# Top-k attention followed by a low-rank mixer: the division by the row sums made on transposed values, with the inverse sums passed through DRAM

## The chip, the cores and the metric

The kernel runs on one core of a Trainium2 chip. A core has five engines, each with its own in-order queue: TensorE (PE, matmuls and transposes; PEld is its weight load), VectorE (DVE), ScalarE (ACT), GpSimd (POOL) and SyncE (SP, which here only issues DMAs). They meet through semaphores. Data lies in SBUF (128 partitions), matmul results in PSUM, inputs and outputs in DRAM. The metric is the device time of one execution in microseconds (us); lower is better.

## The reference

Batch 8, 8 heads, 576 positions, head size 64, everything fp32. Attention keeps the 32 largest scores of each row; its output, with the heads side by side, goes through a mixer over positions (rank 32 between U and V) and a two-layer MLP.

```
scores = scale * np.matmul(q, k.transpose(0, 1, 3, 2))
kth = np.partition(scores, -top_k, axis=-1)[..., -top_k:-top_k + 1]
scores = np.where(scores >= kth, scores, -1000000000.0)
scores = scores - np.max(scores, axis=-1, keepdims=True)
attn = np.exp(scores)
attn = attn / (np.sum(attn, axis=-1, keepdims=True) + 1e-09)
o = np.matmul(attn, v)

x = o.transpose(0, 2, 1, 3).reshape(B, S, H * D)
h = x.transpose(0, 2, 1) @ U @ V
u = x + h.transpose(0, 2, 1)
out = u + np.maximum(u @ w_ch1, 0.0) @ w_ch2
```

w_ch1 is 512 x 2048 and w_ch2 is 2048 x 512.

## The kernel before

Two heads make a pair `g`: 4 pairs per batch, 32 in all. The 576 rows of a pair are five row tiles: t = 0 to 3 of 128 rows (`MAIN` = 512) and a tail, t = 4 (`NT`), of 64 rows, in which both heads share one tile (head 0 in partitions 0 to 63, head 1 in 64 to 127). The first four pairs (g < `NPAIR`) take five steps, one per tile; from pair 4 on a pair takes four steps, and the last of them holds t = 3 and the tail.

Each tile passes through these stages, spread over four successive steps:

- `scores` (TensorE, L332 and for the tail L364; ScalarE copies into `Ssb` at L377 to L400), `fold` and `split`, which make from each row two shorter ones (`pair`: GpSimd sum at L428, VectorE maximum at L430, GpSimd difference at L431).
- `front`: VectorE finds the 32nd largest value by MAX8 and MATCH_REPLACE8 (L481 to L516). Then ScalarE and GpSimd (L542 to L546) push all smaller scores far down, and ScalarE takes the exponential and, with it, the row sums (`weigh`, L435). The row sums of a pair are the columns of `den`: rows are partitions, and the nine columns are 4 tiles x 2 heads and the tail. 1e-9 is added at L556.
- The probabilities are turned. From pair 6 on (`shared`) the main tiles go through `blocks`: VectorE transposes 32x32 blocks into `y` (L572), SyncE writes `y` to DRAM (`away`, L578), and `back` reads it as `PT` on ScalarE's queue (L587). Tails are turned by TensorE (`turns`, L608 and L613).
- `values`: TensorE multiplies by v. For t < 4 the result has features in partitions and rows in columns (`O`, L646 and L649; ScalarE copies it into `XT` at L658). For the tail the rows stay in partitions (L633), and ScalarE scales both halves by the inverse row sum on the way into `x` (L641).
- `mixed`, once per pair: TensorE turns `XT` back to rows (L672), ScalarE copies to `x` (L676), GpSimd multiplies by the inverse row sums (L677, `den4`), TensorE multiplies by U into `pT` (L688), ScalarE copies it (`Tb`, L696), then for two parts of the columns TensorE multiplies by V (L700) and adds `x` by turning it onto the same PSUM tile (L702). ScalarE copies the sum into `uT` (L710), which has features in partitions. `inverse` (L621) makes the reciprocal on VectorE.

When the fourth pair of a batch is mixed, `mlp(b)` is put on the list of fillers: first layer L742, with the ReLU copy `hT` at L755, second layer L760, `uT` added on GpSimd at L772, and the result turned back (L784) and written out (L790). The last batch goes through `closing`, a second way to make the same products with fewer matmuls (L829 to L1041), which runs after all attention work.

The order on every engine is written out by hand: the loop at the end of the kernel goes through the steps and calls parts of `front` (a generator), `scores`, `values` and so on. `fill()` stands between them some seven times a step; each call moves `mixed` by one `yield` and then issues MLP matmuls until a fixed share of work (`share`, in units of matmul columns) is paid out. `mixed(g, None, 1)` waits one `fill`, does the first part, and goes on in the next step.

PSUM tiles come from three pools of two buffers: `ps_s` (scores), `ps_m` (MLP) and `ps_t` (`O`, `tp`, `pT`, `up`). A DMA's completion is counted on one of eight semaphores, and the build makes a DMA wait until the earlier DMA on its semaphore has landed, whichever queue issued that.

Of the kernel before, what the change touches and what calls it, by code (L numbers as in the profile page):

```python
# [8 lines left out]
F32 = mybir.dt.float32  # L9
# [3 lines left out]
ALU = mybir.AluOpType  # L13
# [13 lines left out]
def kernel(  # L27
# [28 lines left out]
    nc = tc.nc  # L56
    B, H, S, D = q.shape
    P = 128
# [4 lines left out]
    NT, TAIL = 4, 64  # L63
    MAIN = NT * P
    HALF = S // 2
    assert S == MAIN + TAIL and D == 64 and H % 2 == 0 and C == 512 and TOPK % 8 == 0
    NPAIR = H // 2
    NP = B * NPAIR

    CH = NT + 1  # L70
    ALONE = NPAIR * CH
# [4 lines left out]
    BLK = 32  # L76
# [4 lines left out]
    const = ctx.enter_context(tc.tile_pool(name="const", bufs=1))  # L81
# [22 lines left out]
    vds = [const.tile([P, P], F32, name=f"vd{i}") for i in range(NV)]  # L104
    vts = [const.tile([P, 2, D], F32, name=f"vt{i}") for i in range(NV)]

    xs = [const.tile([P, NT + 1, P], F32, name=f"x{i}") for i in range(2)]
    for i in range(NV):
        nc.gpsimd.memset(vds[i], 0.0)
        nc.gpsimd.memset(vts[i], 0.0)  # L110
    for x in xs:
        nc.gpsimd.memset(x[:, NT, :], 0.0)
    W1Q = F // NT
    w1s = [const.tile([P, NC, W1Q], F32, name=f"w1{i}") for i in range(NT)]
    w2 = const.tile([P, NF, C], F32, name="w2")
    U = const.tile([P, NT + 1, R], F32, name="U")

    V = const.tile([NT * R, S], F32, name="V")
    four = const.tile([P, 1], F32, name="four")
    nc.vector.memset(four, -4.0)  # L120

# [8 lines left out]
    def cols(t):  # L130
        return slice(t * P, t * P + rows(t))

    def at(t):
        return slice(OFF[t], OFF[t] + rows(t))

    def half(h):
        return slice(h * D, (h + 1) * D)
# [96 lines left out]

    raw, qkTs, S2s, uTs, XTs, dens = {}, {}, {}, {}, {}, {}
    probs, PTs, folds, fronts_of = {}, {}, {}, {}
    inverted, aways = set(), {}

    def load(g):

# [376 lines left out]
    def inverse(g, lo, hi):  # L617
        den = dens[g][:, lo:hi]
        if g == NPAIR - 1:
            nc.vector.tensor_scalar_add(den, den, 1e-9)  # L620
        nc.vector.reciprocal(den, den)  # L621

    def values(g, t):

        PT = PTs.pop((g, t))
        va, vd, vt = (a[g % NV] for a in (vas, vds, vts))
        O = ps_t.tile([P, P], F32, tag="tp", name="O")
        if t == NT:
            den, x = dens[g], xs[g % 2]
            if g not in inverted:  # L630
                inverse(g, 2 * NT if g == NPAIR - 1 else 0, 2 * NT + 1)
            for j in range(NT + 1):
                nc.tensor.matmul(  # L633
                    O,
                    lhsT=PT[:, j],
                    rhs=va[:, :, j, :] if j < NT else vt,
                    start=(j == 0),
                    stop=(j == NT),
                )
            for h in range(2):  # L640
                nc.scalar.mul(x[half(h), NT, half(h)], O[half(h), half(h)], den[half(h), 2 * NT :])  # L641
            return
        if shared(g, t):
            PT = PT.rearrange("p c n -> p (c n)")
            PT = PT.rearrange("p (a c j) -> p c a j", a=4, j=BLK)
        nc.tensor.matmul(O, lhsT=vd, rhs=PT[:, 2 * NT], start=True, stop=False)  # L646
        for j in range(NT):
            for h in range(2):
                nc.tensor.matmul(  # L649
                    O[half(h)],  # L650
                    lhsT=va[:, h, j, :],
                    rhs=PT[:, NT * h + j],
                    start=False,
                    stop=(j == NT - 1),
                )
        if t == 0:
            XTs[g] = attn.tile([P, MAIN], F32, tag="XT", name="XT", bufs=1)
        nc.scalar.copy(XTs[g][:, cols(t)], O)  # L658


    def mixed(g, wait, lag=0):

        for _ in range(lag):
            yield
        b, gi = divmod(g, NPAIR)
        if gi == 0:
            uTs[b] = mlpp.tile([P, NC, S], F32, tag="uT", name="uT")
        XT, den = XTs.pop(g), dens[g]
        X = xs[g % 2]
        tp = ps_t.tile([P, NT, P], F32, tag="tp", name="tp")  # L670
        for t in range(NT):
            nc.tensor.transpose(tp[:, t, :], XT[:, cols(t)], ident)  # L672
        X4 = X[:, 0:NT, :].rearrange("p t (h d) -> p t h d", h=2)
        tp4 = tp.rearrange("p t (h d) -> p t h d", h=2)
        den4 = den[:, 0 : 2 * NT].rearrange("p (t h) -> p t h ()", h=2).to_broadcast([P, NT, 2, D])
        nc.scalar.copy(X4, tp4)  # L676
        nc.gpsimd.tensor_tensor(X4, X4, den4, ALU.mult)  # L677
        if wait is None:
            waiting.append(g)
            while g in waiting:  # L680
                yield
        else:
            for _ in range(wait):
                yield
        pT = ps_t.tile([P, P], F32, tag="tp", name="pT")
        for t in range(NT + 1):
            i = t % NT * R
            nc.tensor.matmul(  # L688
                pT[i : i + R, :],
                lhsT=U[:, t, :],  # L690
                rhs=X[:, t, :],
                start=(t < NT),
                stop=(0 < t),
            )
        Tb = mlpp.tile([P, P], F32, tag="Tb", name="Tb")
        nc.scalar.copy(Tb, pT)  # L696
        yield
        for chunks, (lo, hi) in zip(PARTS, SPAN):
            up = ps_t.tile([P, WIDE], F32, tag="tp", name="up")
            nc.tensor.matmul(up[:, 0 : hi - lo], lhsT=Tb, rhs=V[:, lo:hi], start=True, stop=False)  # L700
            for t in chunks:
                nc.tensor.matmul(  # L702
                    up[:, OFF[t] - lo : OFF[t] - lo + rows(t)],
                    lhsT=X[:, t, :],
                    rhs=ident if t < NT else ident2,
                    is_transpose=True if t < NT else None,
                    start=False,
                    stop=(t == chunks[-1]),
                )
            nc.scalar.copy(uTs[b][:, gi, lo:hi], up[:, 0 : hi - lo])  # L710
            yield
        if gi == NPAIR - 1:
            fillers.append(closing(b) if b == B - 1 else mlp(b))
# [343 lines left out]
    STEPS = len(steps)  # L1057
# [27 lines left out]
    def tiles(n):  # L1085

        return steps[n] if 0 <= n < STEPS else []

    def weighted(m):

        for g, t in reversed(tiles(m)):
            values(g, t)
        if tiles(m)[-1][1] == NT:
            mixing.append(mixed(g, None, 1) if m < STEPS - 1 else mixed(g, 5, 0))
# [6 lines left out]
    def turned(n):  # L1101

        for g, t in tiles(n):
            yield from turns(g, t)
# [9 lines left out]
    for n in range(STEPS + 2):  # L1114
# [99 lines left out]
        turn()  # L1214
        fill()
        next(last, None)
        next(here, None)
        next_params(1)
        fill()
        if n >= STEPS:  # L1220
            weighted(n - 2)
        elif n - 2 >= ALONE and len(tiles(n - 2)) > 1:
            g2 = steps[n - 2][0][0]
            inverted.add(g2)
            inverse(g2, 0, 2 * NT + 1)
        next(here, None)
        bound = tiles(n + 1)[:1] == [(NPAIR + 1, 0)]
        if not bound:
# [7 lines left out]
        for tile_ in tiles(n - 1):  # L1236
            if shared(*tile_):
                blocks(*tile_)
        turning = turned(n - 1)
        if n < STEPS and t < 2 and g + 1 < NP:  # L1240
            if t == 0:
                coming = loading(g + 1)
            next(coming)
# [41 lines left out]
```

## Time and profile before

| | us |
|---|---|
| three runs | 1685.37, 1685.62, 1686.76 |
| median | 1685.62 |
| the profiled execution | 1686.28 |
| its span (first to last instruction) | 1684.5 |
| TensorE busy | 1586.0 (94%) |
| VectorE busy | 1543.7 (92%) |
| ScalarE busy | 1000.1 (59%) |
| GpSimd busy | 939.0 (56%) |
| mean of the 16 DMA engines, over the span | 107 GB/s |

The profile was taken from one execution. Its page gives busy time by engine, the span in 40 slices with the granted TensorE clock, and the chain of waits followed back from the last instruction; the trace behind it can be asked for any stretch, for one engine's timeline, or for the instructions of one line. A row of a timeline is: start, length, engine, line, operation, output <- inputs, number of merged instructions, and in brackets the idle time before with what ended it. "PEq", "SPq", "ACTq" are the engines' queues issuing a DMA or waiting. In the profile one fp32 matmul shows as two MATMUL records, and a transpose as one.

The span falls into four parts: up to about 280 us the first batch, with the weights being unpacked; from there to about 1540 us the pairs 4 to 31, four steps each; then the rest of the MLP before; and from 1570 us `closing`.

### The profile page before, as it was taken

The page shows a single profiled execution, that of the slowest core. Times are in us where ns is not written, and L with a number is a line of the kernel's source. Part 1 is how long each engine was busy: PE and PEld are TensorE (multiplying, and loading weights), DVE is VectorE, ACT ScalarE, POOL GpSimd, SP SyncE. Part 2 cuts the span into 40 slices and gives each one's busy share as a digit, 9 for nine tenths or more (in the row PEclk, how much of TensorE's full clock was granted, in tenths as well). Part 3 has the DMA queues.
Part 4 walks back from the last instruction along what each step waited for, and adds up shares of the span by engine and source line. Part 5 has one row for each costly group of instructions (what it writes and reads, how often), then busy time and mean ns, then how long its engine had stood idle before and what let it go on. Part 6 is the DMA issues. An engine that isn't in the chain of part 4 may idle for free.

```text
span 1684.5 us, 29512 instructions
## 1 busy us (share of the span) xinstructions
PE 1586.0 (94%) x9498; PEld 1213.4 (72%) x9498; DVE 1543.7 (92%) x4364; ACT 1000.1 (59%) x2475; POOL 939.0 (56%) x741
## 2 busy tenths in 40 slices
PE   4666799999899999999999999999999999999999
PEld 2444466788677887788777887778777887778876
DVE  7999998999999999999999999999999999994452
ACT  4888778665665656565665656565665656554320
POOL 4778668655555555555555555555555455552620
PEclk7788799999999999999999999999999999999999
DMA  3323232254545555554545555554545455533001
GB/s 87 96 75 96 58 91 73 55 133 123 131 110 136 125 131 128 131 129 120 128 117 130 125 130 125 132 125 125 128 115 131 122 134 124 131 105 102 10 1 29
DMA packets 273898, 180.97 MB, mean 107 GB/s; under 512 B 171376, under 2 KB 258256, under 8 KB 273744
## 3 DMA queue, kind: packets, MB, share of 16 engines
q1 hardware_dynamic: 257712, 117.49, 30.2%
q10 hardware_dynamic: 16032, 61.61, 11.7%
q8 instruction: 75, 1.23, 0.3%
q14 instruction: 79, 0.65, 0.1%
HBM read 108.23 MB, written 70.78 MB: 106 GB/s over the span
## 4 chain that ended last, share of the span: by engine, by line
PE 54%; DVE 32%; SPq 4%; DMA 4%; issue 2%; POOL 2%; ACT 1%; DVEq 0%; ACTq 0%; POOLq 0%
PE mm L760 16%; PE mm L742 16%; DVE m L516 10%; DVE upper L511 9%; PE sc L332 4%; PE O L649 4%; DVE first L498 3%; PE mm L836 3%; DVE y L572 3%; DVE upper L483 2%; PE sc L836 2%; PE tp L836 2%; DVE place L511 2%; DMA ld<-in_k_dram 2%; SPq L255 2%
## 5 line engine op out<-in xcount | busy, mean ns | idle before, releaser
L742 PE MATMUL mm<-uT,w 128*128 128x320 f32 (+1 forms) x1792 | 461.1, 410 | 1.9 <-ACT hT L755 1.9
L760 PE MATMUL mm<-hT,w 128*128 128x320 f32 (+1 forms) x1792 | 461.5, 408 | 0.0
L546 POOL TENSOR_TENSOR Ssb<-Ssb,E 128x576 f32<-128x576 f32 x243 | 339.4, 1416 | 210.7 <-ACT E L545 210.4
L742 PEld LDWEIGHTS mm<-uT,w 128*128 128x128 f32 x1792 | 333.7, 191 | 97.5 <-issue 12.0
L760 PEld LDWEIGHTS mm<-hT,w 128*128 128x128 f32 x1792 | 330.5, 190 | 90.3 <-issue 10.2
L516 DVE MAX8 m<-upper 128x8 f32<-128x304 f32 (+1 forms) x780 | 367.4, 512 | 0.7
L511 DVE MATCH_REPLACE8 upper<-m,upper 128x304 f32<-128x304 f32 (+1 forms) x520 | 259.9, 507 | 0.0
L431 POOL TENSOR_TENSOR lower<-lower,upper 128x576 uint32<-128x576 uint32 x108 | 152.3, 1410 | 157.5 <-DVE upper L430 152.6
L428 POOL TENSOR_TENSOR lower<-Ssb 128x576 uint32<-128x576 uint32 x108 | 152.4, 1411 | 144.0 <-ACT Ssb L377 87.0
L435 ACT ACTIVATE Ssb<-Ssb,nmax 128x576 f32<-128x576 f32 x258 | 200.8, 780 | 22.3 <-POOL Ssb L522 10.1
L332 PE MATMUL sc<-qkT 64*128 64x288 f32 (+1 forms) x1056 | 178.8, 460 | 10.8 <-ACT Ssb L386 7.8
L545 ACT ACTIVATE E<-Ssb,least 128x576 f32<-128x576 f32 x243 | 176.2, 768 | 4.2
L483 DVE MAX8 upper<-lower 128x8 f32<-128x288 f32 x432 | 172.2, 440 | 6.9 <-POOL lower L431 6.9
L377 ACT COPY Ssb<-sc 128x576 f32<-128x576 f32 x216 | 127.6, 643 | 69.2 <-PE sc L332 69.1
L572 DVE STREAM_TRANSPOSE y<-Ssb 128x512 f32<-128x512 f32 (+1 forms) x312 | 155.4, 547 | 8.8 <-ACT Ssb L435 8.8
L755 ACT ACTIVATE hT<-mm 128x320 f32<-128x320 f32 (+1 forms) x224 | 92.1, 411 | 112.2 <-PE mm L742 107.4
L649 PE MATMUL O<-PT,va 128*64 128x128 f32 x2048 | 145.1, 286 | 0.0
L332 PEld LDWEIGHTS sc<-qkT 64*128 64x128 f32 (+1 forms) x1056 | 95.7, 197 | 51.2 <-issue 16.4
L649 PEld LDWEIGHTS O<-PT,va 128*64 128x64 f32 x2048 | 113.8, 141 | 16.3 <-issue 1.6
L511 DVE MATCH_REPLACE8 upper<-first,upper 128x304 f32<-128x304 f32 x216 | 97.7, 460 | 0.0
L481 DVE MATCH_REPLACE8 lower<-upper,lower 128x288 f32<-128x288 f32 x216 | 94.1, 444 | 0.0
L430 DVE TENSOR_TENSOR upper<-sc,Ssb 128x576 f32<-128x576 f32 x108 | 80.3, 744 | 12.7 <-ACT Stail L397 12.4
(250 smaller groups left out, 2201.3 us busy)
## 6 DMA issues: line engine op xcount, KB each, us to landing
away<-y SPq DMA_DIRECT2D x416, 144.0 KB, 2.5
PT<-away ACTq DMA_DIRECT2D x104, 576.0 KB, 3.9
raw<-in_moe_w_ch_dram SPq DMA_DIRECT2D x32, 512.0 KB, 3.8
va<-in_v_dram SPq DMA_DIRECT2D x64, 128.0 KB, 2.6
out_dram<-ob SPq DMA_DIRECT2D x59, 128.0 KB, 2.5
ld<-in_q_dram SPq DMA_DIRECT2D x108, 64.0 KB, 3.1
ld<-in_k_dram SPq DMA_DIRECT2D x108, 64.0 KB, 2.6
ld<-in_q_dram SPq DMA_DIRECT2D x108, 8.0 KB, 3.2
```

The lines of the kernel that those rows point to most:

```text
L332: nc.tensor.matmul(out, lhsT=qkT[half(h), 0, cols(t)], rhs=qkT[half(h), 1, lo:hi], start=True, stop=True,)
L428: nc.gpsimd.tensor_tensor(bottom, a.bitcast(U32), b.bitcast(U32), ALU.add)
L435: nc.scalar.activation(E, chunk, AF.Exp, bias=nmax, scale=SCALE, accum_out=total)
L483: nc.vector.max(spot, lower)
L511: nc.vector.match_replace(nxt, ms[c], curs[c], NEG)
L516: nc.vector.max(ms[c], curs[c])
L545: nc.scalar.activation(gap, chunk, AF.Relu, bias=least[:, c : c + 1], scale=-WIDEN)
L546: nc.gpsimd.tensor_tensor(chunk, chunk, gap, ALU.subtract)
L572: nc.vector.transpose(y[:, :, i * NT : i * NT + c].rearrange("p r c j -> p c r j"), E2[:, a : a + c * P].rearrange("p (c r j) -> p c r j", ...
L649: nc.tensor.matmul(O[half(h)], lhsT=va[:, h, j, :], rhs=PT[:, NT * h + j], start=False, stop=(j == NT - 1),)
L742: nc.tensor.matmul(ph[:, 0:w], lhsT=first_layer(cc, f), rhs=uT[:, cc, lo:hi], start=(cc == 0), stop=(cc == NC - 1),)
L760: nc.tensor.matmul(po[:, 0:w], lhsT=w2[:, f, c * P : (c + 1) * P], rhs=hTs[f][:, 0:w], start=(f == 0), stop=(f == NF - 1),)
```

## The change

Nothing changes for pairs 0 to 3, except that `x` and `Tb` have one buffer in place of two. From pair 4 on:

- `inverse` is called half a step sooner, at the end of the step after the pair's last one (behind `blocks`). VectorE writes the nine reciprocals into a tile `upright` of 32 columns and transposes it in 32x32 blocks, so that each sum's 128 values lie along a row; SyncE writes the four blocks to DRAM (`rd`, 9 x 128).
- `scale`, in the next step between two parts of `front`, reads `rd` back on ScalarE's queue in four DMAs, each value repeated over the 64 partitions of its head's features: `sc` has features in partitions and the rows' inverse sums in columns.
- The tail's values are made with features in partitions too: ten matmuls of 64 columns in place of five of 128, copied into the last 64 columns of `XT`.
- `mixed` first multiplies `XT` by `sc` into `uT` on GpSimd (three products), then, two `yield`s later, turns the products on TensorE, the tail by a transpose of its own.
- X isn't added by TensorE any more: the product with V is copied by ScalarE into `sc`, and GpSimd adds it to `uT`.

```diff
+    X = const.tile([P, NT + 1, P], F32, name="x")
+    upright = const.tile([P, BLK], F32, name="upright")
+    nc.vector.memset(upright, 0.0)
...
@@ -618,7 +619,33 @@
         den = dens[g][:, lo:hi]
         if g == NPAIR - 1:
             nc.vector.tensor_scalar_add(den, den, 1e-9)
-        nc.vector.reciprocal(den, den)
+        if g < NPAIR:
+            nc.vector.reciprocal(den, den)
+            return
+        inverted.add(g)
+        nc.vector.reciprocal(upright[:, 0 : 2 * NT + 1], den)
+        turned_ = small.tile([P, BLK], F32, tag="rows", name="rows", bufs=1)
+        nc.vector.transpose(turned_, upright)
+        rd = dram.tile([2 * NT + 1, P], F32, tag="rd", name="rd")
+        scales[g] = rd
+        for a in range(4):
+            nc.sync.dma_start(
+                rd[:, a * BLK : (a + 1) * BLK], turned_[a * BLK : a * BLK + 2 * NT + 1]
+            )
+
+    def scale(g):
+
+        rd = scales.pop(g)
+        sc = attn.tile([P, S], F32, tag="scale", name="scale", bufs=1)
+        scales[g] = sc
+        for h in range(2):
+            nc.scalar.dma_start(
+                sc[half(h), 0:MAIN].rearrange("p (t n) -> p t n", t=NT),
+                rd[0 : 2 * NT].rearrange("(t h) n -> h t n", h=2)[h : h + 1].to_broadcast([D, NT, P]),
+            )
+            nc.scalar.dma_start(
+                sc[half(h), MAIN:S], rd[2 * NT : 2 * NT + 1, half(h)].to_broadcast([D, TAIL])
+            )
     def values(g, t):
@@ -626,7 +653,19 @@
         va, vd, vt = (a[g % NV] for a in (vas, vds, vts))
         O = ps_t.tile([P, P], F32, tag="tp", name="O")
         if t == NT:
-            den, x = dens[g], xs[g % 2]
+            if g >= NPAIR:
+                for j in range(NT + 1):
+                    for h in range(2):
+                        nc.tensor.matmul(
+                            O[half(h), 0:TAIL],
+                            lhsT=va[:, h, j, :] if j < NT else vt[:, h, :],
+                            rhs=PT[:, j, half(h)],
+                            start=(j == 0),
+                            stop=(j == NT),
+                        )
+                nc.scalar.copy(XTs[g][:, MAIN:S], O[:, 0:TAIL])
+                return
+            den = dens[g]
             if g not in inverted:
                 inverse(g, 2 * NT if g == NPAIR - 1 else 0, 2 * NT + 1)
             for j in range(NT + 1):
@@ -638,7 +677,7 @@
                     stop=(j == NT),
                 )
             for h in range(2):
-                nc.scalar.mul(x[half(h), NT, half(h)], O[half(h), half(h)], den[half(h), 2 * NT :])
+                nc.scalar.mul(X[half(h), NT, half(h)], O[half(h), half(h)], den[half(h), 2 * NT :])
             return
         if shared(g, t):
             PT = PT.rearrange("p c n -> p (c n)")
@@ -654,7 +693,7 @@
                     stop=(j == NT - 1),
                 )
         if t == 0:
-            XTs[g] = attn.tile([P, MAIN], F32, tag="XT", name="XT", bufs=1)
+            XTs[g] = attn.tile([P, S], F32, tag="XT", name="XT", bufs=1)
         nc.scalar.copy(XTs[g][:, cols(t)], O)
@@ -666,15 +705,35 @@
         if gi == 0:
             uTs[b] = mlpp.tile([P, NC, S], F32, tag="uT", name="uT")
         XT, den = XTs.pop(g), dens[g]
-        X = xs[g % 2]
+        uT = uTs[b][:, gi]
+        if g >= NPAIR:
+            sc = scales.pop(g)
+            pairs_ = [
+                a[:, 0:MAIN].rearrange("p (b n) -> p b n", b=2) for a in (XT, sc)
+            ]
+            ends = [uT[:, OFF[t] : OFF[t] + 2 * P] for t in (0, 2)]
+            for i, end in enumerate(ends):
+                nc.gpsimd.tensor_tensor(end, pairs_[0][:, i], pairs_[1][:, i], ALU.mult)
+            nc.gpsimd.tensor_tensor(uT[:, at(NT)], XT[:, MAIN:S], sc[:, MAIN:S], ALU.mult)
+            yield
+            yield
         tp = ps_t.tile([P, NT, P], F32, tag="tp", name="tp")
         for t in range(NT):
-            nc.tensor.transpose(tp[:, t, :], XT[:, cols(t)], ident)
-        X4 = X[:, 0:NT, :].rearrange("p t (h d) -> p t h d", h=2)
-        tp4 = tp.rearrange("p t (h d) -> p t h d", h=2)
-        den4 = den[:, 0 : 2 * NT].rearrange("p (t h) -> p t h ()", h=2).to_broadcast([P, NT, 2, D])
-        nc.scalar.copy(X4, tp4)
-        nc.gpsimd.tensor_tensor(X4, X4, den4, ALU.mult)
+            nc.tensor.transpose(
+                tp[:, t, :], XT[:, cols(t)] if g < NPAIR else uT[:, at(t)], ident
+            )
+        X4 = X[:, 0:NT, :]
+        nc.scalar.copy(X4, tp)
+        if g < NPAIR:
+            X4 = X4.rearrange("p t (h d) -> p t h d", h=2)
+            den4 = den[:, 0 : 2 * NT].rearrange("p (t h) -> p t h ()", h=2)
+            nc.gpsimd.tensor_tensor(X4, X4, den4.to_broadcast([P, NT, 2, D]), ALU.mult)
+        else:
+            if g == NPAIR:
+                nc.gpsimd.memset(X[TAIL:P, NT, :], 0.0)
+            tp = ps_t.tile([P, P], F32, tag="tp", name="tp")
+            nc.tensor.transpose(tp[0:TAIL], uT[:, at(NT)], ident)
+            nc.scalar.copy(X[0:TAIL, NT, :], tp[0:TAIL])
         if wait is None:
             waiting.append(g)
             while g in waiting:
@@ -692,13 +751,15 @@
                 start=(t < NT),
                 stop=(0 < t),
             )
-        Tb = mlpp.tile([P, P], F32, tag="Tb", name="Tb")
+        Tb = mlpp.tile([P, P], F32, tag="Tb", name="Tb", bufs=1)
         nc.scalar.copy(Tb, pT)
         yield
         for chunks, (lo, hi) in zip(PARTS, SPAN):
             up = ps_t.tile([P, WIDE], F32, tag="tp", name="up")
-            nc.tensor.matmul(up[:, 0 : hi - lo], lhsT=Tb, rhs=V[:, lo:hi], start=True, stop=False)
-            for t in chunks:
+            nc.tensor.matmul(
+                up[:, 0 : hi - lo], lhsT=Tb, rhs=V[:, lo:hi], start=True, stop=(g >= NPAIR)
+            )
+            for t in chunks if g < NPAIR else ():
                 nc.tensor.matmul(
                     up[:, OFF[t] - lo : OFF[t] - lo + rows(t)],
                     lhsT=X[:, t, :],
@@ -707,7 +768,11 @@
                     start=False,
                     stop=(t == chunks[-1]),
                 )
-            nc.scalar.copy(uTs[b][:, gi, lo:hi], up[:, 0 : hi - lo])
+            if g < NPAIR:
+                nc.scalar.copy(uT[:, lo:hi], up[:, 0 : hi - lo])
+            else:
+                nc.scalar.copy(sc[:, lo:hi], up[:, 0 : hi - lo])
+                nc.gpsimd.tensor_tensor(uT[:, lo:hi], uT[:, lo:hi], sc[:, lo:hi], ALU.add)
             yield
         if gi == NPAIR - 1:
             fillers.append(closing(b) if b == B - 1 else mlp(b))
@@ -1088,7 +1153,7 @@
     def weighted(m):
-        for g, t in reversed(tiles(m)):
+        for g, t in tiles(m):
             values(g, t)
         if tiles(m)[-1][1] == NT:
             mixing.append(mixed(g, None, 1) if m < STEPS - 1 else mixed(g, 5, 0))
@@ -1214,15 +1279,16 @@
         turn()
         fill()
         next(last, None)
+        if n < STEPS and n - 2 >= ALONE and len(tiles(n - 2)) > 1:
+            scale(steps[n - 2][0][0])
         next(here, None)
         next_params(1)
         fill()
         if n >= STEPS:
+            if n == STEPS:
+                inverse(NP - 1, 0, 2 * NT + 1)
+                scale(NP - 1)
             weighted(n - 2)
-        elif n - 2 >= ALONE and len(tiles(n - 2)) > 1:
-            g2 = steps[n - 2][0][0]
-            inverted.add(g2)
-            inverse(g2, 0, 2 * NT + 1)
         next(here, None)
         bound = tiles(n + 1)[:1] == [(NPAIR + 1, 0)]
         if not bound:
@@ -1237,6 +1303,8 @@
             if shared(*tile_):
                 blocks(*tile_)
         turning = turned(n - 1)
+        if n < STEPS and n - 1 >= ALONE and len(tiles(n - 1)) > 1:
+            inverse(steps[n - 1][0][0], 0, 2 * NT + 1)
         if n < STEPS and t < 2 and g + 1 < NP:
             if t == 0:
                 coming = loading(g + 1)
```

More of the change, by code (lines that the diff above doesn't have):

```diff
@@ L105 @@
     vts = [const.tile([P, 2, D], F32, name=f"vt{i}") for i in range(NV)]
-    xs = [const.tile([P, NT + 1, P], F32, name=f"x{i}") for i in range(2)]
+    X = const.tile([P, NT + 1, P], F32, name="x")
     for i in range(NV):
@@ L110 @@
         nc.gpsimd.memset(vts[i], 0.0)
-    for x in xs:
-        nc.gpsimd.memset(x[:, NT, :], 0.0)
+    nc.gpsimd.memset(X[:, NT, :], 0.0)
     W1Q = F // NT
@@ L236 @@
     probs, PTs, folds, fronts_of = {}, {}, {}, {}
-    inverted, aways = set(), {}
+    inverted, aways, scales = set(), {}, {}
     def load(g):
```

## The prediction

> **What bounds the kernel now.** I read the stretches first, then the chain of waits, then the timelines of one pair. The columns after the stretch are the busy time of PE, PEld, DVE, ACT and POOL, then the granted clock and the DMA share.
>
> ```profile
> 280.00:600.00 320.00, 312.63 (x1944) 242.07 (x1941) 311.30 (x938) 198.86 (x496) 186.90 (x143) 0.99 0.45 112
> 600.00:1500.00 900.00, 899.60 (x5519) 694.88 (x5519) 879.87 (x2654) 537.07 (x1343) 498.02 (x381) 1.00 0.50 126
> ```
>
> From 600 to 1500 us TensorE never idles (899.6 of 900) and VectorE is busy for 97.8%. The pair period there is 47.5 us (the reciprocal of L621 at 599.99 and, 19 pairs on, at 1502.16), so VectorE needs 46.4 us of each pair and has 1.1 us to spare. TensorE time is kernel time; the fillers are paid out by a fixed share per step, so nothing refills a hole. In 280 to 600 VectorE sets the pace (46.3 us a pair from 366 to 459) and TensorE has slack.
>
> The chain over one pair of that stretch (start, length, what; a fp32 matmul is two records, a transpose one):
>
> ```profile
> 938.67 1.11 PE O L633 x10
> 939.78 0.22 PE O L646 x2
> 940.00 1.02 PE O L649 x16
> 941.03 1.18 PE sc L364 x14
> 942.21 1.17 PE sc L332 x8
> 943.38 1.06 PE mm L742 x4
> 944.44 0.44 PE tp L672 x4
> ...
> 954.32 0.74 PE up L700 x2
> 955.06 0.39 PE up L702 x4
> ...
> 956.80 0.43 PE up L700 x2
> 957.23 0.22 PE up L702 x2
> ```
>
> It is PE from end to end, and L633 and L702 are what the change touches. GpSimd's timeline at the same place:
>
> ```profile
> 944.25 1.41 POOL L428 TENSOR_TENSOR lower<-Ssb 128x576 uint32<-128x576 uint32 x1 [2.28 <-issue]
> 946.46 1.04 POOL L677 TENSOR_TENSOR x<-x,den 128x512 f32<-128x512 f32 x1 [0.79 <-ACT x L676]
> 947.46 1.41 POOL L431 TENSOR_TENSOR lower<-lower,upper 128x576 uint32<-128x576 uint32 x1
> ...
> 971.85 0.73 POOL L772 TENSOR_TENSOR oT<-oT,uT 128x256 f32<-128x256 f32 x1 [1.50 <-DVE upper L430]
> ```
>
> The division (L677) now comes after TensorE's transposes (944.28), and TensorE wants its result only at 952.5. The change turns this round.
>
> **The change part by part.** A steady pair is one of the 23 pairs 8 to 30; T is the start of the first matmul after the pair's last scores (943.31).
>
> *TensorE, removed.* The five products that add X back (L702): 0.39 + 0.22 = 0.61 us. The tail's values were ten records at 111 ns, 1.11 us; now they are twenty of 64 columns, two halves side by side. Nearest rows: the 64-column passes of L364 start 57 ns apart per pair of halves (0.57 us in all); L649's pace of 109 ns per pair would give 1.09. The passes of L364 have the same moving size, so 0.57. *Added:* the tail's transpose, 0.11 as the 64-wide third transpose of L784 (at most 0.2). Sum: -0.61 - 0.54 + 0.11 = -1.04 us a pair (-0.43 to -1.04).
>
> *TensorE, new wait.* As built, GpSimd's order is L428's sum, then the three products by the scale, then L431's; TensorE's transposes wait for the products. L428 ends at 945.66, T + 2.35, in every steady pair. A 256-column product is 0.73 (L772), a 64-column one 0.32 (the uint32 sums of L188 and L190), each overlapping the next by 0.05 as in L546: done at T + 4.03. TensorE wakes 0.05 later (L688 after L677) and its next matmul follows 0.16 on, as after any exposed weight load (L649's first): T + 4.24. Between the scores and the transposes now stand five matmuls of 320 columns, six of 256, or six of 256 and two transposes, at 0.27 and 0.216 a record plus 0.11 on leaving the scores: T + 2.78, 2.70 or 2.92, and 0.55 for five transposes. Waits: 0.91, 0.91, 0.99, 0.77 in the four kinds of pair, mean 0.90. Bounds: at L677's 2.03 ns per column the products end at T + 3.6 and the wait is 0.5; at L829's 0.94 it is 1.3. I take 0.90, since L772 has the same shape and two whole operands. Queued behind the transposes are the MLP's matmuls; nobody else fills the hole.
>
> The Trainium skill (GPSIMD Engine Reference, 3.1) gives 4497 ns for a two-operand add of 2048 fp32 columns, about 2.2 ns a column; by it a product would be 0.56 us, an estimate, the wait about 0.5 and the change a gain of about 9 us more than my sum says. The same page advises against this engine for elementwise work. L772's 0.73 for 256 columns is the trace's answer, and I go by it.
>
> *ScalarE, read-back.* Two scalings (0.63) become two small copies (about 0.5); no path runs through them. The four DMA issues stand between the second exponential and L502, on a queue whose next work frees a PSUM bank of the first MLP layer:
>
> ```profile
> 933.70 0.21 ACT L502 ACTIVATE nmax<-first 128x2 f32<-128x2 f32 x1
> 934.39 0.38 ACT L755 ACTIVATE hT<-mm 128x256 f32<-128x256 f32 x1 [0.48 <-PE mm L742]
> 936.11 0.38 ACT L755 ACTIVATE hT<-mm 128x256 f32<-128x256 f32 x1 [1.34 <-PE mm L742]
> ```
>
> The last transposes of that pair (L572) end at y = 927.35. SyncE issues the four parts of `away` until y + 1.8 and then the four of the inverse sums at 0.44 each (L578's row); they land 2.5 us after issue (same row), at about y + 5.6. ScalarE arrives at y + 6.35, so it waits for nothing. An issue took 0.33 (L587) to 0.62 (L260); the read-back has many pieces on 64 partitions, nearest to L255 and L287 (0.585 and 0.51), so 0.57, four 2.28: to 935.98. L502 and the copy behind it end at 936.57, the next group has ended at about 936.02, and TensorE wants the bank then: 0.6 us of wait. This holds for the 6 steady pairs with 256-column first-layer work there. In the 320-column pairs the groups end 2.16 us apart and the copy is in time; elsewhere ScalarE copies after long accumulations. Sum 3.6 us, 0 with the short issue, 8 if also the rows land as late as `PT` does (3.9). The scale itself is wanted only 10 us later.
>
> *VectorE.* The reciprocal moves; added is a 128x32 transpose, 0.17 by the slope between L572's 0.27 (128 columns) and 0.69 (512), and up to 0.13 for its wait on the reciprocal: 0.3 a pair. The 1.1 us to spare hide it in steady pairs. In pairs 4 to 7 that cover is missing: 4 x 0.3 = 1.2 us. The earlier reciprocal doesn't wait: ScalarE ends the sums (L556, 971.42) before L572 is done (974.82).
>
> *SyncE.* Four issues, 1.8 us, ahead of q's eight loads, which then end near y + 8.7; the next `away` is due at y + 10. If that cover is gone, `PT` comes late and TensorE waits at L646.
>
> *GpSimd, the rest.* The adds into uT (0.87 and 0.73) fall where L431 waits for VectorE (152.6 us in 65 waits). Only where a batch's first MLP starts with nothing in between, once, does TensorE wait: 0.6 us.
>
> *Last pair.* It gains the 1.04 and pays about 0.5, because its read-back holds ScalarE until about 1547 and a transpose (L613, 1547.26) needs the bank behind it: -0.5.
>
> *Sum* against the profiled execution (1686.28 us, of which the span is 1684.5): 23 x (0.90 - 1.04) = -3.2; +3.6, +1.2, +0.6, -0.5: +1.7 us. The median of the runs shown is 0.7 us lower, 1685.62, so 1687.3; I say 1688.
>
> **The rivals.**
>
> *Faster: the products are done sooner.* For it: L677 did 512 columns in 1.04. Then the wait is 0.5 and 23 x (0.5 - 1.04) = -12.4; with short issues 0 instead of 3.6; and +1.3 as above: 1674.5. Against: L677's second operand is one number per 64 columns. VectorE allows no more than about 1.1 - 0.3 = 0.8 us a pair (18 us, to 1668), so it isn't the cap here.
>
> *Slower: the read-back takes ScalarE's queue.* Place: between the exponential and L502. It decides once the block lasts past y + 8.1, the end of the next group less L502 and a copy; from there every further 0.1 us costs TensorE 0.1. For it: SyncE's rows go as high as 1.7 (L255) and 2.07 (L578) for one issue, and each DMA can wait for an older one on its semaphore. If the rows land at y + 8 and the issues take 0.65, the block ends at y + 10.6, the wait is 2.4 in six pairs, and 0.2 in the six 320-column ones: 16 us, total 1685.6 - 3.2 + 16 + 1.3 = 1700. Against: `away` landed in 2.5 at the median.
>
> *The gain isn't there: the 64-column passes keep the 109 ns pace.* TensorE saves 0.5 a pair less, +12: 1699. Against: L364.
>
> **How the numbers follow.** A difference of 0.2% (3.4 us) is about what a measurement of this kernel can tell from no change. The forecast, that saving and wait nearly cancel, gets 0.47 (its own range 1680 to 1695); of it 0.06 is faster, 0.27 the same, 0.14 slower. Faster rival 0.25; slower rival 0.21, and the rival of the pace 0.07, of which 0.01 is the same. Together: faster 0.31, same 0.28, slower 0.41. The range takes in both sides up to the rivals' times: 1674 to 1702.
>
> **What would show it.** Right: TensorE idle before the transposes of uT of some 0.9 us a pair, released by GpSimd's product; the tail's twenty records in about 0.6; no L702 after the second product with V for pairs from 4 on; TensorE's busy time down by some 29 us and its idle time up by as much. ScalarE's read-back some 2.3 us long, with L502 after it. Wrong: no idle time at those transposes (then the kernel is faster), waits of TensorE on ScalarE's hT copies above 1 us in the step after a pair's end, VectorE idle before its reciprocal, or TensorE waiting on `PT` in most steps.

## The result, and the profile after

The changed kernel takes 1734.12 us (median of four runs, 1731.94 to 1736.78) against 1685.49 for the kernel before on the same chip: a ratio of 1.0288, with a 95% interval of 1.0271 to 1.0306. It is 48.6 us slower. The prediction was 1688, from 1674 to 1702, with "slower" as its likeliest single outcome (0.41) but at a fraction of this size.

The same two stretches as before (after the stretch: busy time of PE, PEld, DVE, ACT and POOL, then clock and DMA share):

```profile
280.00:600.00 320.00, 299.28 (x1885) 224.97 (x1883) 301.48 (x909) 187.62 (x475) 195.03 (x166) 0.98 0.47 117
600.00:1500.00 900.00, 865.44 (x5376) 651.87 (x5376) 844.83 (x2559) 508.25 (x1290) 515.54 (x436) 0.99 0.51 127
```

TensorE was busy without a gap; now it idles for 35 us of 900. But VectorE lost as much: 55 us idle instead of 20. Both wait for something else; the granted clock (1.00 to 0.99) isn't it, since e1 below is as slow at 1.00. The pair period went from 47.5 to 49.7 us (the reciprocals of L626 at 607.00 and, 18 pairs on, at 1500.95). Four of the waits that grew most, over the whole run (total, times, longest); the wait on the products by the scale (L722), also new, was foreseen and is taken up further down:

```profile
PEld mm L807 <- ACT hT L820: 36.7, 27, 4.3
ACT nmax L503 <- DMA ld<-in_q_dram: 31.8, 8, 5.2
DVE qkT L303 <- DMA ld<-in_k_dram: 30.9, 15, 3.7
PE mm L807 <- ACT hT L820: 27.5, 15, 3.9
```

In the kernel before, the third was 5.2 us, the first and the last 3.6 and 1.9, and the second didn't exist. (The weight load and the matmul behind it stand in the same wait, so their times aren't added.) They show two places. The first is ScalarE's queue, where the prediction's slower rival looked; this is the timeline of ScalarE, then of TensorE, at the end of one pair:

```profile
959.25 0.64 ACTq L642 DMA_DIRECT2D scale<-rd  x1
959.92 0.63 ACTq L646 DMA_DIRECT2D scale<-rd  x1
962.99 0.61 ACTq L642 DMA_DIRECT2D scale<-rd  x1
963.64 0.63 ACTq L646 DMA_DIRECT2D scale<-rd  x1
964.31 0.20 ACT L503 ACTIVATE nmax<-first 128x2 f32<-128x2 f32 x1 [5.25 <-DMA ld<-in_q_dram]
964.42 0.64 ACT L820 ACTIVATE hT<-mm 128x256 f32<-128x256 f32 x2
```

```profile
956.25 4.91 PE L807 MATMUL mm<-uT,w 128*128 128x256 f32 x22
964.84 5.41 PE L807 MATMUL mm<-uT,w 128*128 128x256 f32 x12 [3.68 <-ACT hT L820]
```

Two read-backs go out, then the queue stands for 2.4 us until a load of q, issued by SyncE, has landed; L503 and the hT copies stand behind, and TensorE waits 3.68 us for a PSUM bank. The second place is SyncE's queue, here in another pair:

```profile
705.02 1.75 SPq L579 DMA_DIRECT2D away<-y  x4
706.87 1.77 SPq L632 DMA_DIRECT2D rd<-rows  x4
...
710.69 0.70 SPq L261 DMA_DIRECT2D ld<-in_q_dram  x1
713.96 0.58 SPq L256 DMA_DIRECT2D ld<-in_q_dram  x1
...
715.88 1.81 SPq L261 DMA_DIRECT2D ld<-in_q_dram  x1
...
718.91 1.97 SPq L579 DMA_DIRECT2D away<-y  x4
...
725.47 0.62 SPq L261 DMA_DIRECT2D ld<-in_k_dram  x1
```

Between the fourth and the fifth load of q SyncE stands for 2.6 us; the list of its waits puts such gaps at L256 down to `PT` landing (35.0 us in 14 waits from 600 to 1500). The next write of `away`, and k's loads behind it, go out late, and the chain of waits shows who pays:

```profile
720.93 0.59 SPq L256
...
725.47 3.49 DMA ld<-in_k_dram
729.14 1.38 DVE qkT L303
730.52 0.69 DVE upper L484 x2
```

VectorE, with hardly a microsecond to spare per pair, waits for k.

For the experiments I read two numbers from such timelines, as means over the pairs from 600 to 1500 us: how long the queue that issues the read-back is held (first issue to the end of the last), and when the last load of k has been issued, counted from the first issue of the pair's last `away` (SyncE, 705.02, in the pair shown). In the changed kernel they are 3.90 and 20.1 us; in the kernel before the second is 17.5.

### The profile page after: what moved, and what is told of

The parts are those of the page before. It is cut to its first block, busy times and chain, and to the rows that moved or that the text cites. A ratio compares the mean times of both kernels' runs of the same rounds, so it can differ in the third digit from the quotient of the medians.

```text
span 1734.9 us, 30336 instructions
## 1 busy us (share of the span) xinstructions
PE 1584.9 (91%) x9638; PEld 1184.7 (68%) x9638; DVE 1549.0 (89%) x4393; ACT 988.7 (57%) x2475; POOL 999.3 (58%) x853
## 4 chain that ended last, share of the span: by engine, by line
DVE 46%; PE 29%; DMA 8%; SPq 8%; issue 4%; POOL 2%; ACT 2%; ACTq 0%; DVEq 0%; POOLq 0%
DVE m L517 12%; DVE upper L512 11%; PE mm L807 8%; PE mm L825 7%; DVE upper L484 5%; DVE first L499 4%; DVE y L573 4%; DVE lower L482 3%; DMA ld<-in_q_dram 3%; PE mm L901 3%; SPq L256 3%; DVE place L512 2%; DMA ld<-in_k_dram 2%; PE O L688 2%; SPq L261 2%
## 5 line engine op out<-in xcount | busy, mean ns | idle before, releaser
L807 PE MATMUL mm<-uT,w 128*128 128x320 f32 (+1 forms) x1792 | 474.6, 416 | 32.0 <-ACT hT L820 27.5
L807 PEld LDWEIGHTS mm<-uT,w 128*128 128x128 f32 x1792 | 339.2, 194 | 140.3 <-ACT hT L820 36.7
L484 DVE MAX8 upper<-lower 128x8 f32<-128x288 f32 x432 | 172.3, 440 | 9.9 <-POOL lower L432 9.8
L333 PEld LDWEIGHTS sc<-qkT 64*128 64x128 f32 (+1 forms) x1056 | 96.1, 198 | 53.3 <-issue 15.9
```

The costliest lines, as they stand in the source:

```text
L333: nc.tensor.matmul(out, lhsT=qkT[half(h), 0, cols(t)], rhs=qkT[half(h), 1, lo:hi], start=True, stop=True,)
L484: nc.vector.max(spot, lower)
L807: nc.tensor.matmul(ph[:, 0:w], lhsT=first_layer(cc, f), rhs=uT[:, cc, lo:hi], start=(cc == 0), stop=(cc == NC - 1),)
```

## The experiments

| run | median | ratio to before, 95% | queue held | last k |
|---|---|---|---|---|
| the change | 1734.1 | 1.0271 to 1.0306 | ScalarE 3.90 | 20.1 |
| e1_readback_on_synce | 1737.6 | 1.0293 to 1.0328 | SyncE 2.93 | 20.7 |
| e2_no_readback | 1682.3 | 0.9972 to 0.9992 | none | 18.0 |
| e3_no_dram_trip | 1677.8 | 0.9943 to 0.9972 | none | 17.7 |
| e4_before_plus_dmas | 1732.2 | 1.0262 to 1.0292 | ScalarE 4.42 | 20.3 |
| e5_tiny_readback | 1716.0 | 1.0169 to 1.0200 | ScalarE 3.77 | 19.2 |
| e6_readback_on_gpsimd | 1688.1 | 1.0009 to 1.0028 | GpSimd | 18.4 |
| e7_readback_later | 1722.0 | 1.0205 to 1.0239 | ScalarE 4.03 | 19.9 |
| e8_two_dmas | 1714.2 | 1.0154 to 1.0185 | ScalarE 1.14 | 19.4 |
| e10_two_on_gpsimd | 1693.0 | 1.0032 to 1.0056 | GpSimd | 18.4 |
| e11_one_tiny | 1693.0 | 1.0035 to 1.0061 | ScalarE 0.35 | 18.6 |
| e15_writes_behind_q | 1713.8 | 1.0158 to 1.0189 | GpSimd | 18.7 |
| e16_third_fill | 1688.0 | 1.0006 to 1.0022 | GpSimd | 18.3 |
| e18_all_on_gpsimd | 1695.8 | 1.0049 to 1.0073 | GpSimd | 17.9 |
| e19_six_on_gpsimd | 1689.0 | 1.0010 to 1.0030 | GpSimd | 18.2 |
| e20_scalare_held | 1718.4 | 1.0186 to 1.0215 | ScalarE 4.18 | 18.1 |
| e20b_scalare_held_shorter | 1691.6 | 1.0024 to 1.0051 | ScalarE 2.78 | 18.0 |
| e21_three_on_gpsimd | 1688.5 | 1.0009 to 1.0027 | GpSimd | 18.3 |

The runs were made on several chips; the kernel before took 1685.1 to 1685.6 beside each of them.

**Which part costs.** Four runs took the change apart.

```diff
 # e1: in scale(), all four
-            nc.scalar.dma_start(
+            nc.sync.dma_start(
 # e2: scale() only makes the tile; in mixed()
-                a[:, 0:MAIN].rearrange(...) for a in (XT, sc)
+                a[:, 0:MAIN].rearrange(...) for a in (XT, V)
 # e3: as e2, and in inverse()
-        for a in range(4):
-            nc.sync.dma_start(rd[...], turned_[...])
 # e4: the kernel before, with the change's early inverse(), rd and scale() added
+        nc.vector.transpose(turned_, upright)
+        rd = dram.tile([2 * NT + 1, P], F32, tag="rd", name="rd")
...
```

> The change, with the four read-back DMAs per pair issued on SyncE's queue instead of ScalarE's; same place in the program, same result. ScalarE theory (the read-back's four issues, 0.6 us each, and the waits between them hold ScalarE's queue for 3 to 6 us a pair, so that L503 and the hT copies come late): at most 1700, and ScalarE's waits before L503 on a DMA (31.8 us in the changed kernel) are gone. SyncE theory (eight more DMAs a pair on eight semaphores make SyncE's loads wait, and VectorE's qkT waits for k): no better than the changed kernel, 1734 or more, since SyncE now issues four more; VectorE's wait at L303 30 us or more. GpSimd theory (the products by the scale stand in front of TensorE's transposes whatever the DMAs do): 1730 to 1735.

> The change without the four read-back DMAs: XT is multiplied by V (a tile of the same shape that is always there) instead of the inverse sums, so the output lacks the division; the four small writes to DRAM stay. ScalarE theory: 1684 to 1692, what the sum of the prediction gives without the read-back. SyncE theory: half the added DMAs are gone, about 1710. GpSimd theory: 1730.

> As the run before, and the four writes of the inverse sums to DRAM left out too (VectorE still makes and transposes them): the change with no added DMA. ScalarE theory: the same as the run before within 4 us. SyncE theory: 1684 to 1690, some 20 below the run before. GpSimd theory: 1730.

> The kernel before with its own arithmetic, plus the change's added DMAs alone, at the change's places: the reciprocal half a step sooner, a 128x32 transpose on VectorE, four writes to DRAM on SyncE, four read-backs on ScalarE into a tile that nobody uses (one x buffer instead of two, for its room). ScalarE theory and SyncE theory: 1725 to 1740, the whole loss. GpSimd theory: 1685 to 1692.

The arithmetic by itself is a gain: without any added DMA 1677.8, 7.3 us below the kernel before. The four writes cost 4.5 us, the read-back 51.8 (1734.1 - 1682.3), and the DMAs alone, added to the old arithmetic, cost 47. That ends the GpSimd theory. But the ScalarE theory missed e1 by 37 us: with ScalarE out of it SyncE loses as much (VectorE's waits in e1, 600 to 1500 us):

```profile
DVE qkT L303 <- DMA ld<-in_k_dram: 35.0, 12, 3.7
DVE qkT L303 <- DMA va<-in_v_dram: 13.9, 5, 3.7
```

There the loads of q end as in e2 (9.3 us after the first `away`), and the four read-backs, 2.93 us in SyncE's own queue, stand ahead of k. The SyncE theory missed e2 by 28, and e3 fell outside the ranges of all three theories. So neither alone.

**Bytes, number or place.**

```diff
 # e5: four read-backs of 32 numbers, two of them
+            nc.scalar.dma_start(sc[h * D : h * D + 1, 0:BLK], rd[h : h + 1, 0:BLK])
 # e6: in scale(), all four
-            nc.scalar.dma_start(
+            nc.gpsimd.dma_start(
 # e7: the call of scale() moved down, ahead of blocks()
 # e8: rd holds head by head 5 rows, the tail's row twice; in scale(), for each head
+            nc.scalar.dma_start(
+                sc[half(h)],
+                rd[h * (NT + 1) : (h + 1) * (NT + 1)]
+                .rearrange("(o t) n -> o (t n)", o=1)
+                .to_broadcast([D, (NT + 1) * P]),
+            )
```

> The change with its four read-back DMAs a pair at their places, but each brings only 32 numbers of one partition; the products use V (as in e2_no_readback), so the output lacks the division. Two theories are left after the first four runs, which put 52 us on the read-back whichever queue carries it. Order theory: the queue that holds a read-back stands still while it waits for an older DMA on its semaphore (a load of q, PT) and SyncE's loads wait for the read-back in turn; the bytes don't matter: 1712 to 1735. Traffic theory: the 640 packets (288 KB) a pair crowd out PT and the loads of q: 1682 to 1692, as without the read-back.

> The change with the four read-back DMAs on GpSimd's queue, whose DMAs are counted on semaphores of their own; same bytes, same place in the program. Order theory: neither ScalarE nor SyncE stands behind a read-back any more: 1684 to 1700, the rest being what GpSimd loses by issuing. Traffic theory: the same packets at the same time: 1720 to 1735.

> The change with the read-back called some 5 us later in the same step, behind split and ahead of blocks, when the loads of q and PT have landed; still four DMAs on ScalarE. Order theory: the waits for q and PT are gone, four issues of 0.62 remain: 1684 to 1696. Traffic theory: the packets now fall beside the loads of k and v: 1710 to 1735.

> The change with two read-back DMAs a pair in place of four, at the same place: the inverse sums lie head by head in DRAM with the tail's row given to both heads, so that each partition reads one piece of 640 numbers (128 packets a pair instead of 640; 14% more bytes). One more small reciprocal, and the tail's product in two halves. Order theory: half of the waits remain, 1698 to 1720. Traffic theory, where packets count: 1684 to 1694; where bytes count: 1734 or more.

The traffic theory was right about e7 alone. e6 moves the same bytes at the same place for 5.7 us over e2, though in fewer packets (see the end), and e5 loses 34 us with next to no bytes. Nor do the packets slow `PT`: from 600 to 1500 us its last packet ends, in the mean of those issued beside the loads of q, 3.55 us after the issue in e2 and 3.65 in the change and in e5. What the other 18 us between e5 and the change belong to (bytes, packets, or the longer issues) wasn't separated. e5's issues are short (0.27 us in the mean), and yet ScalarE is held as long as with the full ones:

```profile
703.53 0.26 ACTq L642 DMA_DIRECT2D scale<-rd  x1
707.03 0.22 ACTq L643 DMA_DIRECT2D scale<-rd  x1
707.30 0.21 ACT L503 ACTIVATE nmax<-first 128x2 f32<-128x2 f32 x1 [3.70 <-DVE m L517]
```

The fourth waits 3.2 us for an older DMA, in this build `PT`. The releaser named at L503, VectorE, had long been done; the row above shows that the queue came free only at 707.25. Here lies the rule told ahead of the prediction: eight semaphores for all DMAs of SyncE and ScalarE, and each DMA waits for the one eight places before it, whoever issued that. In the built program the read-backs fall among the loads of q and behind `PT`; so ScalarE waits for SyncE's loads or for `PT`, and SyncE's later loads wait for `PT` and for read-backs. GpSimd's DMAs have semaphores of their own. The traces show the order at work: each read-back among the loads of q moves the wait for `PT` one load ahead. It falls on no load of q in e3, on the last of the eight in e2, the seventh in e11 (one read-back), the sixth in e8 (two) and the fifth in the change (of whose four read-backs three lie within the eight places), in most pairs; SyncE's wait there, from 600 to 1500, is 6.0, 15.9, 25.6 and 35.0 us, and k's last load leaves at 18.0, 18.6, 19.4 and 20.1. (The expectation for e11 says that no load of q waited for `PT` in e2; the last one did.) e7 missed the order theory's range by 26: the call stood 5 us later in the text, but the order among the semaphores is fixed at build, and there the read-backs still lay between the loads of q (ScalarE held 4.03 us). e8 holds ScalarE for only 1.14 us and loses 32 all the same.

**The two prices.** These runs separate ScalarE's share from SyncE's.

```diff
 # e20 (six) and e20b (four): e2, and in scale(), with no DMA
+        for _ in range(6):
+            nc.scalar.copy(sc, V)
 # e11: e5 with one read-back
+        nc.scalar.dma_start(sc[0:1, 0:BLK], rd[0:1, 0:BLK])
 # e10: e8 on nc.gpsimd
```

> e2_no_readback with ScalarE held for 3.85 us a pair at the place of the read-back (six copies of 128x576, 0.642 each in the kernel before), with no DMA in it; in the changed kernel ScalarE stood there from 5.6 to 9.6 us after the reciprocal in the mean. The output lacks the division. If the block of ScalarE makes the loss: 1715 or more. If the loss comes by SyncE (the last load of k is issued 18.0 us after the pair's last write of y in e2_no_readback, 20.1 in the changed kernel, and VectorE waits for it at L303): 1683 to 1696, the price of the prediction's slower rival, with k's last load still at 18.

> e20_scalare_held with four copies in place of six: ScalarE is held 2.57 us a pair, about what the read-back's four issues take when none waits (the prediction took 2.28 and a price of 3.6 us for the whole kernel). The output lacks the division. If the loss is in proportion to the time held (36 us for 3.85): 1704 to 1708. If there is a cover of some 2 us, as the prediction had it, and only what lasts longer costs: 1683 to 1694.

> e5_tiny_readback with one read-back DMA a pair in place of four (32 numbers, on ScalarE; products by V; the output lacks the division). In this build the last load of q in 24 pairs follows PT by eight DMAs and so waits for PT to land, which no load of q did in e2_no_readback's steady pairs; ScalarE's own waits are gone. Theory of the issues on ScalarE (the loss grows with the number of issues): a quarter of e5's loss, 1689 to 1692. Theory of the eight semaphores (one more DMA between PT and the last load of q is enough to tie SyncE to PT): 1696 to 1710.

> The two read-back DMAs of e8_two_dmas, issued on GpSimd's queue at the same place. Order theory (two issues of about 0.66 on GpSimd end before it is wanted for L432, and no DMA of the other queues is touched): 1680 to 1686, that is e2_no_readback's 1682 with at most a few us more, against e8's 1714. A theory that the bytes or their landing cost: 1700 or more.

ScalarE: held for 4.18 us a pair, with the loads of k on time, it costs 36 us over e2; held for 2.78, it costs 9. So e20 came out as its first theory said, and the shorter run shows a cover: the line through both crosses zero at about 2.3 us and rises by 19 us per us beyond (28 pairs, 0.7 of each); two points give no more than an estimate. The waits that this hold makes in e20, whole run, are on TensorE and on VectorE:

```profile
PEld mm L801 <- ACT hT L814: 29.8, 26, 3.6
DVE upper L431 <- ACT Stail L398: 22.7, 8, 4.5
DVE upper L484 <- POOL lower L432: 21.3, 9, 3.3
```

SyncE: from e10 to e8 the same two DMAs move from GpSimd to ScalarE, the last k comes 1.0 us later and the time rises by 21. From e2 to e11 it comes 0.56 later (+10.6), from e2 to e1 2.7 later (+55). All three give about 20 us per us. e11 landed between its two ranges, since one DMA moves k by only half a microsecond, but on this line. e10 missed by 7: it is no faster than e6, and its tail's product in two halves shows as a new wait of TensorE's weight loads before the tail's transpose (8.8 us from 600 to 1500), which may be the 5 us over e6; that wasn't tested alone.

By these two prices the change should pay 30 us for ScalarE's 3.90 and 42 for k at 20.1 instead of 18.0; it pays 52, so the prices don't add. e4 pays 47 with ScalarE held for 4.42 and k 2.8 us later than in the kernel before, less than k's price alone, and e7 pays 40, hardly more than k's price, with ScalarE held for 4.03 at a later place. VectorE's waits give a split; these are the change's, then e2's, from 600 to 1500 us:

```profile
DVE qkT L303 <- DMA ld<-in_k_dram: 23.4, 12, 3.7
DVE upper L431 <- ACT Stail L398: 18.8, 4, 5.7
DVE upper L484 <- POOL lower L432: 6.7, 5, 2.5
DVE qkT L303 <- DMA va<-in_v_dram: 5.4, 3, 2.8
```

```profile
DVE qkT L303 <- DMA ld<-in_k_dram: 9.5, 11, 1.5
DVE qkT L303 <- DMA va<-in_v_dram: 4.4, 4, 1.5
```

VectorE idles 40 us more than in e2 (55 against 15). Some 15 of them are for k and v, and 25 stand at the two places where VectorE waits behind the held ScalarE in e20. For the 23 steady pairs (18 in the stretch) that makes some 19 and 32 of the 52 us, an estimate from these waits.

**Is there a version that wins?** With GpSimd carrying the read-back I tried five more.

```diff
 # e15: e10, the call of scale() as in e7, and inverse() behind next(coming)
 # e16: e6, one more yield ahead of the transposes
 # e18: e16, and in inverse()
-            nc.sync.dma_start(
+            nc.gpsimd.dma_start(
 # e19: e18 with e10's two read-backs, and a yield ahead of the tail's transpose
 # e21: e6 with three read-backs: the rows in the order head 0, tail, head 1
+        for h, to, at_, n in ((0, 0, 0, S), (1, 0, (NT + 1) * P, MAIN), (1, MAIN, S, TAIL)):
+            nc.gpsimd.dma_start(
+                sc[half(h), to : to + n], flat[:, at_ : at_ + n].to_broadcast([D, n])
+            )
```

> e10_two_on_gpsimd with the four small writes issued behind the loads of q instead of ahead of them, and the read-back some 5 us later, behind split. If the 4.5 us between e2_no_readback and e3_no_dram_trip are the loads of q being late by four issues: 1677 to 1683, faster than the kernel before. If they are the writes' own places among the semaphores: 1682 to 1690. If the writes now land so late that GpSimd stands: above 1690.

> e6_readback_on_gpsimd with TensorE's transposes of the products one fill later (a third yield), so that the products are done when TensorE comes to them. If TensorE's wait there (27 us from 600 to 1500) is time that the kernel loses: 1668 to 1678. If VectorE sets the pace by now: 1680 to 1688, with the wait gone and VectorE's idle time in 600 to 1500 below 20 us.

> e16_third_fill with the four small writes on GpSimd's queue too, so that the eight semaphores of the other queues are used as in e3_no_dram_trip. If the writes' 4.5 us come by SyncE: 4 to 6 less than e16_third_fill, and the last load of k at 17.7 instead of 18.4. If GpSimd's eight issues (some 4.6 us a pair) delay its sums: 0 to 15 more than e16_third_fill.

> e18_all_on_gpsimd with two read-backs in place of four (as in e10_two_on_gpsimd), and the tail's transpose one more fill later, so that its product in two halves holds nobody. If GpSimd's issues cost: 2 to 6 less than e18_all_on_gpsimd; otherwise the same within 2 us.

> e6_readback_on_gpsimd with three read-backs a pair in place of four (the inverse sums lie head by head in DRAM, with the tail's row between the heads, so that head 0 needs one DMA and head 1 two; the tail's product stays whole). One more small reciprocal on VectorE. If GpSimd's issues are what e6 has over e2_no_readback: 1684 to 1687; if the extra reciprocal or something else outweighs them: 1688 to 1692.

None beats the kernel before. e15's writes land so late that GpSimd stands 51.9 us (600 to 1500) at its read-back. e16 removes TensorE's wait at the transposes (from 600 to 1500 no matmul waits for the products any more, and the weight loads 2.3 us instead of e6's 21.3) and gains nothing; VectorE's idle time stays at 20 us. e18 has k's last load at 17.9, but GpSimd's eight issues make VectorE wait for its sums (16.3 us at L484, 2.4 in e16). e19, with six issues, is back at e6's time, and e21 stays there too. So the trip through DRAM costs at least 10 us on any queue that I tried, and the arithmetic brings 7.

## Why the prediction was wrong

*TensorE removed: right.* The tail's values took 0.68 us from start to start and 0.58 on the chain of waits (before 1.11, predicted 0.57), and L702 is gone. *The new wait: right in its place and size.* GpSimd and TensorE in the pair whose T is 974.36:

```profile
975.30 1.41 POOL L429 TENSOR_TENSOR lower<-Ssb 128x576 uint32<-128x576 uint32 x1 [2.51 <-issue]
976.67 1.44 POOL L716 TENSOR_TENSOR uT<-XT,scale 128x256 f32<-128x256 f32 x2
978.06 0.33 POOL L717 TENSOR_TENSOR uT<-XT,scale 128x64 f32<-128x64 f32 x1
```

```profile
974.36 2.86 PE L807 MATMUL mm<-uT,w 128*128 128x256 f32 x12
977.47 0.44 PE L722 MATMUL tp<-ident,uT 128*128 128x128 f32 x2 [0.25 <-POOL uT L716]
...
978.59 1.68 PE L807 MATMUL mm<-uT,w 128*128 128x256 f32 x7
```

The products are done at T + 4.03, as predicted, and TensorE goes on with the MLP at T + 4.23 (predicted 4.24; within 0.05 of it in every pair from 600 to 1500). But the wait isn't lost time, as e16 shows: taking it away gains nothing. That VectorE sets the pace by then fits its idle time, but TensorE also waits for hT instead in e16 (8.3 us against e6's 1.1), so it isn't shown alone. It is, I think, why e3 came out 5.4 us better than this part of the sum (-1.9); it was not tested further, nor were the small terms for pairs 4 to 7, the first MLP and the last pair.

*ScalarE, read-back: here it failed.* "ScalarE arrives at y + 6.35, so it waits for nothing" took only the landing of the rows as a reason to wait, and priced four issues, 2.28 us, at 3.6 us in all. The issues took 0.61 each, near the 0.57, and a hold of that length would have cost little (e20b: 9 us at 2.78). But in most pairs the third or fourth of them waited for `PT` or a load of q on its semaphore, and the hold became 3.90 us in the mean (2.6 to 6.0). TensorE's waits on the hT copies above 1 us, which the prediction named as a sign of being wrong, are there (3.68). The slower rival named this very wait and priced it at 16 us, in six pairs and a little in six more; held alone it costs some 30 by the line through e20 and e20b, because in the other pairs too the copies of the scores stand behind it, and VectorE's folds behind them (the waits of e20).

*SyncE: the second failure.* Four issues were counted and priced at nothing, with a cover of y + 8.7 against y + 10. The four writes alone cost 4.5 us (e3 to e2) and brought the last load of q eight places behind `PT`; it ended 9.26 us after the first `away`, and in the change 11.75, because the read-backs had brought the fifth load to that place. The sentence on what happens "if that cover is gone" named `PT` and L646; it was k's loads and VectorE at L303, the engine that had 1.1 us to spare (28.8 us of waits for k and v from 600 to 1500, 14 in e2). An edit on ScalarE's queue was never followed into SyncE's loads.

*VectorE and the products with V on GpSimd* stayed hidden, as said: e3 holds both and is faster than before. The rival of the pace (109 ns) fell with the 0.68 us, and the faster rival fell with the products: they took 0.74 us each, as the forecast had it (0.73), and not the shorter time that this rival needed. That its 1674.5 lies near e3's 1677.8 is luck.

The Trainium skill (DMA: Bandwidth & Descriptors, "Issuing engines are not separate DMA queues") says that starting DMAs from several engines saves only the sequencer's time to start them, which is usually small beside the DMA itself. In this kernel the choice of the queue was worth 46 us for the same bytes (e6 against the change), because the queues wait for each other by the semaphores.

## What to carry to other kernels

A DMA added to a tuned kernel must be placed twice: in the queue that issues it, with all that stands behind it there, and in the order in which DMAs share completion semaphores, where it moves the waits of other queues' loads. Before calling a few issues hidden, follow that order for one period, and ask of each load that gets a slower neighbour who reads it and how much that engine has to spare. Here VectorE had 1.1 us per period to spare and TensorE none.

## What the hardware showed unasked

The same read-back left fewer and larger packets on GpSimd's queue: 96 a pair (64 of 4096 bytes and 32 of 1024, without the 4-byte ones) against 640 on ScalarE's (512 of 512 and 128 of 256). The list of queues, for the change and then for e6 (packets, MB, share of 16 engines):

```profile
q10 hardware_dynamic: 35744, 69.88, 13.4%
```

```profile
q10 hardware_dynamic: 16032, 61.61, 11.3%
q0 software_dynamic: 4480, 8.26, 2.4%
```

An issue held GpSimd about as long as ScalarE: 0.65 us in the mean for the larger read-back and 0.54 for the smaller, against 0.62 and 0.61.
